# Channel attention over a 384 x 384 x 384 image: 374 rows kept instead of 372, the last folded group in two pieces of three

## The chip, the cores and the metric

The kernel runs on one core of a Trainium2 chip. A core has five engines, each with its own instruction stream: TensorE (PE, matrix products), VectorE (DVE, elementwise work), ScalarE (ACT, functions of one input), GpSimd (POOL) and SyncE (SP), which here does nothing but issue transfers. Transfers between the chip's memory and the on-chip SBUF run on 16 DMA engines. The metric is the device time of one execution in microseconds; the number given is the median of several runs.

## The reference

`x` is `1 x 384 x 384 x 384` in bf16 and `w1d` has one element.

```
g = einsum("bhwc->bc", x) / (H * W)      # mean over all pixels, per channel
s = sigmoid(g * w1d[0])                  # 384 numbers
return x * s[:, None, None, :]
```

All of `x` (113 MB) has to be read before the first output value is known, and 113 MB have to be written. SBUF is far smaller than `x`, so most of `x` has to be read a second time, unless some of it stays in SBUF from the first pass to the second.

## The kernel before

**Layout.** The 147,456 pixels are cut into 1152 *rows* of 128 pixels; a row is 128 partitions x 384 channels, 98,304 bytes (96 KiB). SBUF holds an *arena* of 275 such rows (`ROWS`). In pass one all 1152 rows are loaded and TensorE adds each into one accumulator by a product with a matrix of ones (`sum_rows`, L280). Then ScalarE makes `s` from it (L503). In pass two each row is multiplied by `s` (`scale`, L517) and stored (L531); the rows that no longer lie in SBUF are loaded again (L274).

**Rows kept.** `N_KEPT` rows needn't be loaded again. Some lie in the arena as they are (*raw* rows, `N_RAW`). The others lie *folded*: four blocks of q rows are packed into three, because a part of the bits of each bf16 number is the same throughout. `GROUPS` lists the groups as (first arena row, q). A group of q takes 4q rows when it is loaded and 3q once `fold` is through, and the q rows at its top come free. `fold` handles a *piece* of p rows per block: two tests on ScalarE that the numbers are packable (L352, reading the scratch rows `Y` that VectorE fills), and ten VectorE instructions (L315 on one operand, L321 on two, with the scratch rows `T`). Pass two undoes it with `unfold`: `fields`, `three` and `fourth`, L315 and L321 again, followed by the scaling. One group (`BANKED`, q = 6) spends the time between in TensorE's accumulator memory. The last one, `EXTRA`, lies at A = 220 with q = 4, in one piece. From W = 232 on, up to the end of the arena, come raw rows; `T` and `Y`, the last 16, are raw rows too once all folds are done. U (108 to 115) and V (212 to 219) are the tops of the last groups of the two columns, raw as well.

**Order of pass one.** It is written out by hand, and SyncE, TensorE, ScalarE and VectorE each follow it. `stream_all` loads rows that are only summed; `take` loads a group's rows; `BETWEEN` puts streamed rows between the groups. After the last group, `EXTRA`, come the streamed rows of `LATE`, then the raw rows that stay (`take_raw`). A load waits until the rows that it overwrites are no longer needed: for streamed rows until TensorE has summed them, for the freed top of a group until `fold` has read it, for `T` and `Y` until the last fold is through.

**Padding.** `hold` makes an engine wait several times for a semaphore that has already been reached. `N_DVE = (62, 14)` puts 62 such instructions (two waits each) at the head of VectorE's stream and 14 ahead of the end of pass one; `N_SP = 20` puts 20 into SyncE's stream.

**Order of pass two.** A small planner (the loop from L771) lays out the instructions while the program is built: it steps a clock of 0.05 us with prices for a row's transfer (0.2267 us), for latencies and for VectorE's instructions, and writes down what each engine would do next. `landed` first holds the raw rows for VectorE, `alongside` those that GpSimd scales in the meantime (13 rows: 4, 4 and 5). Rows that have been stored are free (`idle`) and are loaded with streamed rows, the largest free stretch first. `order` is the order in which the groups are unfolded: the last of the first column, then EXTRA, then the one before the last of the first column, and so on. A group can start if its column has no other group in work (`free`) and if the rows at its top (`TOPS`) are free; the tops of the next two groups in line are not loaded (`N_NEAR`). The first two groups are stored in two parts if q is 8 (`apart`). What comes out is a fixed order per engine, with waits on semaphores; on the chip SyncE issues strictly in that order.

Of the kernel before, what the change touches and what calls it, by code (L numbers as in the profile page):

```python
# [145 lines left out]
def kernel(  # L146
# [13 lines left out]
    B, H, W, C = x.shape  # L160
# [11 lines left out]
    PIECE = 4  # L172
    PAIR = 2 * PIECE
    PAIRS = 4
    U = 3 * PIECE + PAIRS * 3 * PAIR
    G0 = U + PAIR
    V = G0 + PAIRS * 3 * PAIR
    A = V + PAIR
    N_A = 39
    T = A + N_A  # L180
    Y = T + 2 * PIECE
# [3 lines left out]
    FIRST = 0  # L185
    GROUPS = [(0, PIECE)]
    COLUMNS = ([FIRST], [])
    for i in range(PAIRS):
        for column, a in zip(COLUMNS, (3 * PIECE, G0)):
            column.append(len(GROUPS))  # L190
            GROUPS.append((a + 3 * PAIR * i, PAIR))
    BANKED = len(GROUPS)
    GROUPS.append((A, 6))
    EXTRA = len(GROUPS)
    GROUPS.append((A, PIECE))
    W = A + 3 * PIECE
    PS = 3 * GROUPS[BANKED][1]
    N_BANKED = 4 * GROUPS[BANKED][1] + 1
    N_RAW = ROWS - W + 2 * PAIR
# [2 lines left out]

    pieces = [
        (g, lo, min(m, q - lo))
        for g, (_, q) in enumerate(GROUPS) for m in [q if g == BANKED else PIECE] for lo in range(0, q, m)
    ]

    ones = pool.tile([P, P], bf16, name="ones")
# [51 lines left out]
    def raw(a):  # L260

        return c_raw + (a - U if a < G0 else PAIR + a - V if a < A else 2 * PAIR + a - W)

# [104 lines left out]
            join(w2, w2, flat(T + i * p, p), XOR, wc[2] + rows(T + i * p, p), wc[2])  # L368


    N_DVE, N_SP = (62, 14), 20

    fl.add("ACT", lambda: nc.scalar.dma_start(out=w_bf[:], in_=w1d.to_broadcast((1, 1))), writes=["w_bf"], dma=True)
    fl.add("DVE", lambda: nc.vector.memset(ones[:], 1.0), writes=["ones"])  # L374
# [35 lines left out]
    def take(g, lo=0, hi=None):  # L410

        a, q = GROUPS[g]
        hi = (N_BANKED if g == BANKED else 4 * q) if hi is None else hi
        load(c_group[g] + lo, a + lo, hi - lo)
        return sum_rows(a + lo, hi - lo)
# [16 lines left out]
    for i, bk in enumerate(banks):  # L432
        lo, hi = i * BANK, min((i + 1) * BANK, PS * C)
# [4 lines left out]
    S1, S2, S3 = ([slot] for slot in SLOTS)  # L438
# [9 lines left out]
    def group(g, where):  # L448

        if isinstance(where, list):  # L450
            take(g)
            for k in of_group(g):
                fold(k)
            stream_all(where)
        else:
            k1, k2 = of_group(g)
            take(g, 0, 12)
            take(g, 24, 32)
            fold(k1)
            stream_all(where[0])  # L460
            take(g, 12, 24)
            fold(k2)
            stream_all(where[1])

    LATE = [(W + 4, 8), (U, 8), (W + 12, 8), (W + 20, 7)]
    BETWEEN = [
        (2, LOW_COLUMN + HIGH), (4, [(A, 38)]),
        (5, [(G0 - 24, 24), (A - 24, 24), *S1]),
        (6, (S2, S3 + S1)), (7, ([(A - 24, 24)] + S2, S3 + S1)),
        (8, (S2 + S1, [(U, 8)] + S3)), (EXTRA, LATE),  # L470
    ]
    between = sum(n for _, b in BETWEEN for w in b for _, n in (w if isinstance(w, list) else [w]))
    first = N_STREAM - between
# [18 lines left out]
        load(raw(a), a, n)  # L492
        return sum_rows(a, n)

    for a, n in [(V, 8), *LATE, (W, 4), (T, 4), (T + 4, 4), (Y, 4), (Y + 4, 2), (Y + 6, 2)]:
        step = take_raw(a, n)
        if a == Y - 4:
            fl.hold("DVE", 2 * N_DVE[1], step)
# [144 lines left out]
    landed = deque()  # L643
# [45 lines left out]
        return f  # L689


    for a, n, end in ((Y, 2, True), (Y + 2, 2, True), (Y + 4, 4, True), (U, 4, True), (U + 4, 4, True), (T, 8, True), (V, 8, True)):
        landed.append((a, raw(a), n, end))
    landed.append((W, raw(W), 8, True))
    landed.append((W + 8, raw(W + 8), 6, True))


    alongside = deque()
    t = 1.0
    for a, n in ((A + 26, 4), (A + 30, 4), (A + 34, 5)):  # L700
        scale(a, n, "POOL", after=[copied])
        t += 0.2 + 0.84 * n
        alongside.append((t, a, raw(a), n))


    (c0, c1), N_NEAR = COLUMNS, 2
    order = [c0[-1], EXTRA, c0[-2], c1[-1], BANKED, c0[-3], c1[-2], c0[-4], c1[-3], FIRST, c1[-4]]
    line = deque(order)
    home = {g: i for i, column in enumerate(COLUMNS) for g in column}
    home[BANKED], home[EXTRA] = 2, 3  # L710
# [60 lines left out]
    while True:  # L771

        if dve_at <= now:
# [4 lines left out]
            if landed and (ahead < PENDING or not can):  # L778
                a, at, n, end = landed.popleft()
# [13 lines left out]
        if alongside and alongside[0][0] <= now:  # L793
            _, a, at, n = alongside.popleft()
# [3 lines left out]
        while waiting and waiting[0][0] <= now:  # L798
            _, n, then, at, a, known = waiting.popleft()
# [10 lines left out]
        if bank_at is None and len(line) <= total - BANKS_AT and got and max(got)[0] >= N_BANKED:  # L810
            a = max(got)[1]
# [11 lines left out]
        if got and todo < N_STREAM:  # L823
            n, a = max(got)
# [60 lines left out]
```

## Time and profile before

| | |
|---|---|
| Median of 3 runs | 719.24 us (718.77 to 719.4) |
| The profiled execution's own time | 718.83 us |
| its span, first to last instruction | 717.1 us |
| moved by the DMA engines | 303.31 MB |
| read, written | 189.92 MB, 113.25 MB |
| VectorE busy | 475.2 us |
| TensorE busy | 213.0 us |
| ScalarE busy | 121.4 us |
| GpSimd busy | 10.2 us |
| s is ready in SBUF | 269.2 us after the start of the span |

The profile's page begins with the busy time of each engine, then cuts the span into 40 equal slices and gives for each the busy share of the engines, of the DMA engines, and the rate that they moved. Other views used below: the busy time of each engine in chosen stretches (windows), the instructions in order of time (timeline), the groups of equal instructions by line and shape with the mean duration of one (nanoseconds), the chain of work that ended last, and the instructions of one source line, for transfers with the time from issue to landing. "128x1536" is four rows wide, since a row has 384 elements per partition; 768 KB in the transfer view are eight rows.

### The profile page before, as it was taken

How to read it: one execution, taken by the hardware profiler on the slowest of the kernel's cores; microseconds unless marked ns; L12 is line 12 of the kernel's file. 1: busy time of each engine (PE TensorE's matmuls, PEld its weight loads, DVE VectorE, ACT ScalarE, POOL GpSimd, SP SyncE). 2: the span in 40 equal slices, each digit the busy share in tenths (PEclk: the TensorE clock that was granted, in tenths of full speed). 3: DMA queues.
4: the chain of work that ended last, by engine and by line, in shares of the span. 5: the costliest groups of instructions: out<-in, count | busy, mean ns of one | idle time of the engine just before them, and what ended most of it. 6: DMA issues, size and time to landing. Idle time of an engine off the chain costs nothing.

```text
span 717.1 us, 2040 instructions
## 1 busy us (share of the span) xinstructions
PE 213.0 (30%) x1186; PEld 0.3 (0%) x3; DVE 475.2 (66%) x355; ACT 121.4 (17%) x97; POOL 10.2 (1%) x7
## 2 busy tenths in 40 slices
PE   4776978998869780000000000000000000000000
PEld 0000000000000000000000000000000000000000
DVE  4606280639896829999999999779966960128900
ACT  3704160426674610000110000000000000000000
POOL 0000000000000005000000000000000000000000
PEclk9998989999999996555555555555555555555555
DMA  9999999999999989999999999999999999999997
GB/s 373 436 426 440 424 442 426 439 429 420 428 430 425 427 358 355 406 424 431 433 428 422 444 424 445 423 439 428 439 420 435 433 433 436 436 432 431 437 421 343
DMA packets 21038, 303.31 MB, mean 423 GB/s; under 512 B 2338, under 2 KB 2850, under 8 KB 9378
## 3 DMA queue, kind: packets, MB, share of 16 engines
q1 hardware_dynamic: 21024, 303.18, 99.1%
q8 instruction: 4, 0.07, 0.0%
q14 instruction: 8, 0.07, 0.0%
q10 hardware_dynamic: 2, 0.00, 0.0%
HBM read 189.92 MB, written 113.25 MB: 423 GB/s over the span
## 4 chain that ended last, share of the span: by engine, by line
DMA 56%; DVE 23%; PE 7%; another core or an unknown queue 3%; ACT 2%; POOL 1%; SPq 1%; issue 0%; DVEq 0%
DMA arena<-in_x_dram 45%; DVE arena L517 17%; DMA out_dram<-arena 11%; PE bank L280 7%; DVE arena L315 4%; ACT arena L352 2%; DVE arena L321 2%; POOL arena L517 1%; SPq L274 1%; SPq L531 0%; ACT s_bf L503 0%; ACT bank L507 0%; ACT bank L429 0%; DVEq L124 0%
## 5 line engine op out<-in xcount | busy, mean ns | idle before, releaser
L517 DVE TENSOR_TENSOR arena<-arena,s_bf 128x6144 bf16<-128x6144 bf16 (+13 forms) x67 | 226.9, 3424 | 86.1 <-DMA arena<-in_x_dram 71.0
L280 PE MATMUL bank<-arena,ones 128*128 128x384 bf16 x1151 | 207.2, 342 | 46.2 <-DMA arena<-in_x_dram 45.6
L315 DVE TENSOR_SCALAR arena<-arena 128x1536 uint16<-128x1536 uint16 (+4 forms) x193 | 136.9, 763 | 107.6 <-DMA arena<-in_x_dram 94.9
L352 ACT ACTIVATE arena<-arena 128x3072 uint16<-128x3072 uint16 (+1 forms) x38 | 107.6, 2831 | 111.6 <-DVE arena L315 111.6
L321 DVE TENSOR_TENSOR arena<-arena 128x1536 uint16<-128x1536 uint16 (+3 forms) x81 | 106.3, 1312 | 8.4 <-PE bank L280 5.2
L597 PE MATMUL bank<-odd,ones 128*128 128x1 bf16 x1 | 0.2, 184 | 262.2 <-DVE odd L592 262.2
L429 ACT COPY arena<-bank 128x512 uint32<-128x512 uint32 (+3 forms) x9 | 4.4, 497 | 86.6 <-DMA out_dram<-arena 86.3
L517 POOL TENSOR_TENSOR arena<-arena,s_bf 128x1536 bf16<-128x1536 bf16 (+1 forms) x3 | 9.9, 3345 | 269.2 <-ACT bank L507 269.2
L517 DVE TENSOR_TENSOR arena<-arena,bank 128x1536 bf16<-128x1536 bf16 (+3 forms) x8 | 9.4, 1248 | 0.0
L429 ACT COPY bank<-arena 128x512 uint32<-128x512 uint32 (+3 forms) x9 | 4.1, 489 | 26.5 <-PE bank L280 26.5
L352 ACT ACTIVATION_READ_ACCUMULATOR arena<-arena 128x1 f32 x38 | 7.1, 186 | 0.0
L280 PE MATMUL bank<-zeros,ones 128*128 128x384 bf16 x32 | 5.5, 326 | 0.0
L503 ACT ACTIVATE s_bf<-bank,w_sc 128x384 bf16<-128x384 f32 x1 | 0.6, 580 | 13.6 <-PE bank L280 13.6
L294 PE MATMUL bank<-arena,ones 128*128 128x384 bf16 x1 | 0.5, 477 | 7.1 <-DMA arena<-in_x_dram 7.1
L853 ACT ACT_TABLE_LOAD x1 | 1.3, 1283 | 0.7 <-PEq L869 0.7
L384 DVE TENSOR_SCALAR w_sc<-bank 128x1 f32<-128x1 f32 x1 | 0.2, 159 | 1.4 <-PE bank L379 1.4
L379 PE MATMUL bank<-w_bf,ones 1*128 1x1 bf16 x1 | 0.2, 183 | 2.4 <-DMA w_bf<-in_w1d_dram 2.4
L374 DVE MEMSET ones<- 128x128 bf16 x1 | 0.2, 165 | 1.0 <-SPq L118 1.0
L601 DVE CAST odd_i<-bank 128x1 int32<-128x1 f32 x1 | 0.2, 159 | 0.3 <-PE bank L597 0.3
L507 ACT COPY bank<-s_bf 128x192 uint32<-128x192 uint32 x1 | 0.3, 323 | 0.0
L597 PEld LDWEIGHTS bank<-odd,ones 128*128 128x128 bf16 x1 | 0.1, 102 | 521.0 <-DVE odd L592 521.0
L587 DVE TENSOR_REDUCE worst<-seen 128x1 f32<-128x38 f32 x1 | 0.2, 184 | 0.0
(8 smaller groups left out, 0.9 us busy)
## 6 DMA issues: line engine op xcount, KB each, us to landing
arena<-in_x_dram SPq DMA_DIRECT2D x18, 4608.0 KB, 31.8
out_dram<-arena SPq DMA_DIRECT2D x9, 4608.0 KB, 34.5
out_dram<-arena SPq DMA_DIRECT2D x7, 3072.0 KB, 23.6
arena<-in_x_dram SPq DMA_DIRECT2D x5, 3072.0 KB, 15.2
arena<-in_x_dram SPq DMA_DIRECT2D x13, 1152.0 KB, 17.1
arena<-in_x_dram SPq DMA_DIRECT2D x6, 2304.0 KB, 20.1
arena<-in_x_dram SPq DMA_DIRECT2D x15, 768.0 KB, 7.7
arena<-in_x_dram SPq DMA_DIRECT2D x2, 4128.0 KB, 38.2
```

The lines of the kernel that those rows point to most:

```text
L274: lambda: nc.sync.dma_start(out=arena[:, a : a + hi - lo, :], in_=view(xf, *run)[:, lo:hi, :]),
L280: return pe.add_instruction(mybir.InstMatmult(name=nc.get_next_instruction_name(), ins=[pe.lower_ap(rhs), pe.lower_ap(ones[:])], outs=[pe. ...
L294: return nc.tensor.matmul(acc, lhsT=ones[:], rhs=arena[:, i, :], start=first, stop=last)
L315: lambda: nc.vector.tensor_scalar(out=dst, in0=src, scalar1=s0, scalar2=s1, op0=op0, op1=op1),
L321: "DVE", lambda: nc.vector.tensor_tensor(out=dst, in0=a, in1=b, op=op), reads=reads, writes=writes
L352: lambda: nc.scalar.activation(out=y, in_=y, func=ACTF.Copy, accum_out=seen[:, 2 * k + i : 2 * k + i + 1]),
L429: "ACT", lambda: nc.scalar.copy(dst.bitcast(u32), src.bitcast(u32)), reads=reads, writes=writes
L503: lambda: nc.scalar.activation(out=s_bf[:], in_=acc, func=ACTF.Sigmoid, scale=w_sc[:, 0:1]),
L507: "ACT", lambda: nc.scalar.copy(s_ps.bitcast(u32), s_bf[:].bitcast(u32)), reads=["s_bf"], writes=["bank0"]
L517: lambda: vec.tensor_tensor(out=v, in0=v, in1=s[:, None, :].to_broadcast([P, n, C]), op=Op.mult),
L597: lambda: nc.tensor.matmul(votes, lhsT=ones[:], rhs=odd[:], start=True, stop=True),
L853: nc.scalar.preload_act_table(ACTF.Sigmoid)
```

## The change

EXTRA gets q = 6: 24 rows are loaded for it, 18 stay. It is folded in two pieces of three rows, and unfolded in two. The rows it frees are W to W + 5, with W = 238. The arena's raw rows become 53 (59 before), folded rows 320 (312), so 374 rows are kept (372) and 778 are loaded twice (780). In pass one EXTRA's rows come in three loads (9, 6 and 9) with eight streamed rows ahead of the last; LATE has 23 streamed rows instead of 31. The raw rows of W are loaded as 4 and 2. In pass two the first raw rows scaled are in another order, W ahead of T, U and V; GpSimd scales 15 rows, in three instructions of five; and EXTRA comes third in line instead of second. VectorE's first hold has 50 instructions instead of 62.

```diff
+    LAST_GROUP = 6
     BANKED = len(GROUPS)
     GROUPS.append((A, 6))
     EXTRA = len(GROUPS)
-    GROUPS.append((A, PIECE))
-    W = A + 3 * PIECE
+    GROUPS.append((A, LAST_GROUP))
+    W = A + 3 * LAST_GROUP
...
-        for g, (_, q) in enumerate(GROUPS) for m in [q if g == BANKED else PIECE] for lo in range(0, q, m)
+        for g, (_, q) in enumerate(GROUPS) for m in [{BANKED: q, EXTRA: q // 2}.get(g, PIECE)] for lo in range(0, q, m)
...
-    N_DVE, N_SP = (62, 14), 20
+    N_DVE, N_SP = (50, 14), 20
...
             k1, k2 = of_group(g)
-            take(g, 0, 12)
-            take(g, 24, 32)
+            q = GROUPS[g][1]
+            take(g, 0, 3 * q // 2)
+            take(g, 3 * q, 4 * q)
             fold(k1)
             stream_all(where[0])
-            take(g, 12, 24)
+            take(g, 3 * q // 2, 3 * q)
             fold(k2)
             stream_all(where[1])
 
-    LATE = [(W + 4, 8), (U, 8), (W + 12, 8), (W + 20, 7)]
+    LATE = [(U, 8), (W + 6, 8), (W + 14, 7)]
...
-        (8, (S2 + S1, [(U, 8)] + S3)), (EXTRA, LATE),
+        (8, (S2 + S1, [(U, 8)] + S3)), (EXTRA, (LATE[:1], LATE[1:])),
...
-    for a, n in [(V, 8), *LATE, (W, 4), (T, 4), (T + 4, 4), (Y, 4), (Y + 4, 2), (Y + 6, 2)]:
+    for a, n in [(V, 8), *LATE, (W, 4), (W + 4, 2), (T, 4), (T + 4, 4), (Y, 4), (Y + 4, 2), (Y + 6, 2)]:
...
-    for a, n, end in ((Y, 2, True), (Y + 2, 2, True), (Y + 4, 4, True), (U, 4, True), (U + 4, 4, True), (T, 8, True), (V, 8, True)):
+    for a, n, end in ((Y, 2, True), (Y + 2, 2, True), (Y + 4, 4, True), (W, 4, True), (W + 4, 2, True), (T, 8, True), (U, 8, True)):
         landed.append((a, raw(a), n, end))
-    landed.append((W, raw(W), 8, True))
-    landed.append((W + 8, raw(W + 8), 6, True))
+    landed.append((V, raw(V), 8, True))
...
-    for a, n in ((A + 26, 4), (A + 30, 4), (A + 34, 5)):
+    for a, n in ((A + 24, 5), (A + 29, 5), (A + 34, 5)):
...
-    order = [c0[-1], EXTRA, c0[-2], c1[-1], BANKED, c0[-3], c1[-2], c0[-4], c1[-3], FIRST, c1[-4]]
+    order = [c0[-1], c0[-2], EXTRA, c1[-1], BANKED, c0[-3], c1[-2], c0[-4], c1[-3], FIRST, c1[-4]]
```

## The prediction

> **What bounds the kernel.** The page comes first: who is busy, and all the time or in stretches?
>
> ```profile
> span 717.1 us, 2040 instructions
> PE 213.0 (30%) x1186; PEld 0.3 (0%) x3; DVE 475.2 (66%) x355; ACT 121.4 (17%) x97; POOL 10.2 (1%) x7
> ...
> DMA  9999999999999989999999999999999999999997
> GB/s 373 436 426 440 424 442 426 439 429 420 428 430 425 427 358 355 406 424 431 433 428 422 444 424 445 423 439 428 439 420 435 433 433 436 436 432 431 437 421 343
> ```
>
> The DMA engines are busy in every slice, VectorE in two thirds of the span: the bound is bytes over the rate of the DMA engines. Only the first slice, slices 15 to 17 and the last fall off. I opened those by windows: per line the stretch, its length, busy time of PE, PEld, DVE, ACT and POOL, then TensorE's clock, the DMA share and the rate.
>
> ```profile
> 250.00:264.00 14.00, 11.77 (x68) 0.00 (x0) 4.72 (x7) 3.87 (x4) 0.00 (x0) 1.00 1.02 420
> 266.00:268.00 2.00, 1.72 (x10) 0.00 (x0) 0.00 (x0) 0.00 (x0) 0.00 (x0) 1.00 0.24 90
> 268.00:270.00 2.00, 0.55 (x4) 0.00 (x0) 0.80 (x2) 0.90 (x2) 0.39 (x1) 1.00 0.01 4
> 284.00:286.00 2.00, 0.00 (x0) 0.00 (x0) 1.97 (x2) 0.00 (x0) 0.00 (x0) 0.50 0.97 265
> 290.00:292.00 2.00, 0.00 (x0) 0.00 (x0) 2.00 (x2) 0.00 (x0) 0.00 (x0) 0.50 0.99 288
> 292.00:340.00 48.00, 0.00 (x0) 0.00 (x0) 46.69 (x36) 0.00 (x0) 0.00 (x0) 0.50 1.02 425
> 340.00:640.00 300.00, 0.18 (x1) 0.10 (x1) 228.85 (x103) 4.37 (x9) 0.00 (x0) 0.50 1.01 432
> ```
>
> From 266 to past 270 next to nothing moves: pass one has ended, s is being made, the first stores begin. At 284 to 286 and 290 to 292 the engines are busy (0.97, 0.99) and move little; their packets are slow, the queue isn't empty. Everywhere else the queue is full at 420 to 432 GB/s. So an edit changes the time in three ways only: bytes, number of transfers, and places where the queue runs dry.
>
> **Bytes.** 780 streamed rows become 778. A row is 98,304 bytes, at 432 GB/s 0.228 us: two rows, **-0.46 us**. Pass one loads 1152 rows before and after.
>
> **Transfers.** One more load in pass one (EXTRA and LATE 6 for 5, the raw rows 11 as before), one store fewer in the raw rows (11 for 12), one more for the group that is now second in line (32 rows, the last but one of the first column), which is stored in two parts. What a transfer costs in a full queue: 14 us at 420 instead of 432 GB/s lose 0.39 us, over some 7.5 transfers of 8 rows, 0.05 us each. **+0.05 us**, 0 to 0.2 with what the planner may cut otherwise.
>
> **The folds at the end of pass one.** Here is the old EXTRA, one piece of four rows, and what SyncE did after it (timeline, chain, two issues).
>
> ```profile
> 247.16 1.90 DVE L315 TENSOR_SCALAR arena<-arena 128x3072 uint16<-128x3072 uint16 x3 [1.00 <-DMA arena<-in_x_dram]
> ...
> 252.93 1.95 DVE L321 TENSOR_TENSOR arena<-arena 128x1536 uint16<-128x1536 uint16 x2
> 255.95 0.40 issue
> L274 SPq DMA_DIRECT2D arena<-in_x_dram x2: 432/432/433, 258.1 to 258.6; - x2
> DMA to landing us min/median/max: 9.4/9.4/9.4
> ```
>
> It ran from 247.16 to 254.88, 7.7 us. SyncE reached the loads that need it at 255.95, after its end, so the fold was hidden; the last load was issued at 258.6 and landed at 268.0, which shows the depth of the queue. The new pieces have these rows:
>
> ```profile
> L315 DVE TENSOR_SCALAR arena<-arena 128x1536 uint16<-128x1536 uint16 x124 | 62.4, 558 | 5.9 <-ACT arena L352 2.8 <-DMA arena<-in_x_dram 1.6
> L321 DVE TENSOR_TENSOR arena<-arena 128x1536 uint16<-128x1536 uint16 x44 | 42.0, 956 | 0.9
> ...
> L315 DVE TENSOR_SCALAR arena<-arena 128x2304 uint16<-128x2304 uint16 x10 | 7.0, 754 | 0.0
> L321 DVE TENSOR_TENSOR arena<-arena 128x2304 uint16<-128x2304 uint16 x4 | 5.4, 1357 | 0.1
> ```
>
> Two rows more are 0.196 us on L315 and 0.40 on L321, so three rows (no row shows that shape) take 0.46 and 0.755. A piece: 0.754 + 6 x 0.46 + 1.357 + 2 x 0.755 = 6.4 us, with gaps 6.6; it is bounded by 7.7, the piece of four. What lies ahead of EXTRA has six rows more (the first stretch of streamed rows grows by six, LATE shrinks by eight, EXTRA grows by eight), so all comes 1.4 us later: the first piece's 15 rows land at 248.3, its fold ends at 254.9, the second (landed by 252.2) runs to 261.5 and has read the freed rows at 260.0, two joins earlier. Waiting for that are the loads of W (4 and 2), and behind them on SyncE's queue those of T and Y. 22 rows come from W on, 5.0 us, so in a full queue their turn is at 263.0; taking off 1.4 us from issue to first byte (below), the deadline is 261.6. Slack 1.6 us. **0**; if each piece takes 7.7 us, u is read at 262.2 and 0.6 us are lost. A gain is excluded, for the queue ahead is full already.
>
> **Padding.** VectorE's holds:
>
> ```profile
> L126 DVEq EVENT_SEMAPHORE  x57: 49/50/50, 2.7 to 8.2; - x57
> L126 DVEq EVENT_SEMAPHORE  x11: 49/50/50, 267.0 to 268.0; - x11
> L126 DVEq EVENT_SEMAPHORE  x3: 50/50/50, 268.4 to 268.6; - x3
> ```
>
> They come 0.098 us apart (57 in 5.5 us), but after the one at 268.0 there is a pause of 0.4. The first hold is at the head, where VectorE waits for the first rows in any case: twelve fewer gain nothing. The extra piece brings ten instructions and two or three waits, so the second hold moves by at most one place and keeps the pause inside (it stood at the 12th of 14). **0**; if the pause slipped behind the hold it would lie on the path from s to the first store, 0.4 us. The Trainium skill's page "Runtime: NRT & Kernel Launch", section "Instruction fetch mechanics", says that instructions are refilled in blocks of 256 and that crossing a block is mostly hidden. Here the pause shows that it isn't hidden among short waits; by the page the term would be 0 in either case.
>
> **The start of pass two.** Rows: VectorE's raw rows (eight from the accumulator memory's copy of s), GpSimd's, the first store and the store of T.
>
> ```profile
> 269.68 9.40 DVE L517 TENSOR_TENSOR arena<-arena,bank 128x768 bf16<-128x768 bf16 x8
> ...
> 278.99 1.93 DVE L315 TENSOR_SCALAR arena<-arena 128x1536 uint16<-128x1536 uint16 x3
> L517 POOL TENSOR_TENSOR arena<-arena,s_bf 128x1920 bf16<-128x1920 bf16 x1 | 3.8, 3825 | 0.0
> L517 DVE TENSOR_TENSOR arena<-arena,bank 128x1536 bf16<-128x1536 bf16 x3 | 2.7, 948 | 0.0
> ...
> L517 DVE TENSOR_TENSOR arena<-arena,bank 128x768 bf16<-128x768 bf16 x1 | 0.5, 546 | 0.0
> L531 SPq DMA_DIRECT2D out_dram<-arena x1: 348/348/348, 269.8 to 269.8; - x1
> DMA to landing us min/median/max: 1.8/1.8/1.8
> L531 SPq DMA_DIRECT2D out_dram<-arena x1: 332/332/332, 274.5 to 274.5; - x1
> DMA to landing us min/median/max: 3.6/3.6/3.6
> ```
>
> The first store, two rows, landed in 1.8 us into an empty queue, 0.46 of it bytes: 1.4 us of latency. T's eight rows, issued at 274.5, had 16 rows of VectorE and 4 of GpSimd ahead of them. In the new order 14 rows of VectorE lie ahead and nothing of GpSimd, whose first piece of five is done at 269.6 + 3.8 = 273.4 and which the planner's clock (piece at 5.4, T at 5.3) puts behind T. T is scaled 0.4 us earlier (546 for 948 ns), issued at 274.1, and can land at 274.1 + 1.4 + 1.85 = 277.35. The 14 rows have landed at 274.9 (271.6 for the first two, 12 more at 0.228 plus 0.05 for each of four transfers and 0.3 of waiting for VectorE), and T behind them in a full queue would land at 276.75. The queue is dry for **+0.6 us**; the bounds are 0 (GpSimd's piece gets ahead after all) and 1.0 (the four rows that lay between). The Trainium skill's page "DMA: Bandwidth & Descriptors", section "Anatomy of one DMA", gives about 2.0 us fixed cost per transfer in place of the 1.4; by it this gap would be 1.2 and the whole 0.6 us worse.
>
> Then VectorE runs out. Its 38 raw rows (46 before) end at 277.4, and the unfolding of the last group writes into U, stored only behind 35 rows: 271.2 + 35 x 0.228 + 0.6 + 0.4 = 280.2. It starts there instead of at 278.99, and its first twelve rows are ready at 288, 1.3 us later than before. What hides this: GpSimd's 15 rows (the last five done at 281.1) and V are still in the queue, and the first loads, 11, 8 and 10 rows into W, V and GpSimd's places, fill it up to about 291. **0**, if those loads go out as they did (first at 280.9).
>
> **The smaller ring.** Until the first group's stores are through, streamed rows circle through the free raw rows. They were V (8), 23 behind EXTRA's top and 4 of the group: 35. Now they are 8, 15 and 4: 27, eight rows or 1.8 us of DMA time fewer. And EXTRA's 16 rows (3.6 us) no longer come between; the second in line shares the first's column, and the planner waits until that has been stored. What the queue had in store:
>
> ```profile
> out_dram<-arena SPq DMA_DIRECT2D x3, 768.0 KB, 8.2
> arena<-in_x_dram SPq DMA_DIRECT2D x2, 768.0 KB, 6.8
> ```
>
> Between 292 and 340 eight rows took 6.8 to 8.2 us to land, 1.4 + 1.85 of it their own: 3.5 to 5 us lay ahead of them. Less 1.8 that leaves 2 to 3 us, and VectorE, with no EXTRA to unfold, answers faster to each landing: on the chip nothing but its place in line holds the second group back, so it can begin while the first is still being stored. Following the instructions by hand I find no store issued later than about 2 us before the queue would need it. **0**, bounds 0 and 2.3 (rival two). VectorE's own extra work, 2 x (3 x 0.46 + 2 x 0.755 + 1.06 + 0.46) = 8.8 us for 5.5 of the one piece of four, lies in a stage where it has 71 us to spare (228.85 of 300).
>
> **Sum**: -0.46 + 0.05 + 0.6 = +0.2 us on the profiled execution's 718.83, that is 719.0. This one lies 0.41 below the median of the runs, 719.24, so the forecast of a median is **719.4**; the likeliest case's own range is 718.6 to 720.2.
>
> **Rivals.** *One: the second piece comes too late and the end of pass one stalls.* For it: three joins in this pass waited for TensorE, 5.2 us in all, the longest 2.2 by the view of waits:
>
> ```profile
> DVE arena L321 <- PE bank L280: 5.2, 3, 2.2
> ```
>
> If both new pieces wait so, 4.4 us against a slack of 1.6 give 2.8: **722.2**. Against it: the old EXTRA's join didn't wait, since its rows had been summed. It decides once the freed rows are read after 261.6. *Two: the ring runs dry.* 4.5 us in store, less 1.8 for the rows, 1.3 for the late first group and 3.6 for EXTRA's absence, is -2.2: **721.6**. Against it: the second group isn't held back on the chip. *Three: the saving alone*, no gap at T: **718.8**. *Four: the two slow stretches vanish with the new sizes.* They lose 2 x (432 - 265)/432 = 0.77 and 0.67 us; without them and without the gap 718.83 + 0.41 - 0.41 - 1.44 = **717.4**. No row shows what made them slow.
>
> **Chances.** Forecast 0.56, rival one 0.11, two 0.16, three 0.11, four 0.06. 0.2% is 1.44 us, about what runs of this kernel can tell from no change. The forecast and three lie within it, and so does a tenth of the others; slower are one and two in most of their sizes; faster is four. That gives 0.06 faster, 0.69 same, 0.25 slower. The range takes in four's better half and two's price: 717.8 to 721.9.
>
> **What would show it.** Right: 778 rows streamed (303.1 MB moved for the 303.3 of before); the loads of W issued at about 260 and the last landing still at 268; a dip of about 0.6 us between 274 and 278; VectorE idle from 277 to 280; a DMA share near 1 from 292 to 340. Wrong: windows between 258 and 266 below 400 GB/s (rival one), or idle DMA engines between 285 and 330 (rival two), or a last store that waits for VectorE at the end, where the sizes of the last streamed loads change as well.

## The result, and the profile after

| | before | after |
|---|---|---|
| Median of 6 runs each, us | 719.29 (718.21 to 719.67) | 722.91 (721.58 to 723.65) |
| The profiled execution, us | 718.83 | 721.58 |
| its span, us | 717.1 | 719.8 |
| SyncE's transfers | 146 | 153 |
| moved, MB | 303.31 | 303.11 |

The ratio is 1.0052, 95% interval 1.0039 to 1.0065: slower. Measured twice more, as u_same and u_again below, the changed kernel gave 1.0027 (1.0018 to 1.0037) and 1.0035 (1.0022 to 1.0049). So the change costs 2 to 3.6 us. The first two of these intervals don't overlap: the cost moves by about a microsecond from one set of runs to another, so below, smaller differences between runs of different sets aren't told apart. The page after begins so (span, busy times, share of the DMA engines and rate per slice):

```profile
span 719.8 us, 2071 instructions
PE 214.9 (30%) x1186; PEld 0.3 (0%) x3; DVE 484.3 (67%) x384; ACT 124.6 (17%) x101; POOL 11.6 (2%) x7
...
DMA  9999999999999988999999999999999999999997
GB/s 375 437 427 435 437 426 429 437 433 423 428 429 427 424 333 341 398 421 422 426 436 424 430 442 427 440 426 439 428 436 423 440 431 438 430 432 427 437 428 321
```

Slices 15 to 17 have 333, 341, 398 for 358, 355, 406, and the last 321 for 343; elsewhere the slices scatter by a few GB/s. VectorE has 9 us more to do, but the DMA engines are the bound as before. The windows tell in which stretch the time went. First the kernel before, then the changed one (columns as in the prediction; the last is the rate, the one ahead of it the DMA share):

```profile
270.00:284.00 14.00, 0.00 (x0) 0.00 (x0) 13.93 (x14) 0.00 (x0) 9.56 (x3) 0.60 0.96 390
284.00:292.00 8.00, 0.00 (x0) 0.00 (x0) 7.88 (x7) 0.00 (x0) 0.00 (x0) 0.50 1.01 354
300.00:320.00 20.00, 0.00 (x0) 0.00 (x0) 18.96 (x18) 0.00 (x0) 0.00 (x0) 0.50 1.02 424
320.00:360.00 40.00, 0.00 (x0) 0.00 (x0) 39.53 (x23) 3.95 (x8) 0.00 (x0) 0.50 1.02 429
```

```profile
270.00:284.00 14.00, 0.00 (x0) 0.00 (x0) 11.58 (x13) 0.00 (x0) 11.31 (x3) 0.55 0.92 372
284.00:292.00 8.00, 0.00 (x0) 0.00 (x0) 6.40 (x4) 0.00 (x0) 0.00 (x0) 0.50 0.90 294
300.00:320.00 20.00, 0.00 (x0) 0.00 (x0) 18.73 (x17) 0.00 (x0) 0.00 (x0) 0.50 1.01 413
320.00:360.00 40.00, 0.00 (x0) 0.00 (x0) 34.33 (x32) 0.00 (x0) 0.00 (x0) 0.50 1.01 425
```

Against 432 GB/s a stretch loses (432 - rate) / 432 of its length: 1.36, 1.44, 0.37, 0.28 us before and 1.94, 2.56, 0.88, 0.65 after. The four rows are 0.58 + 1.12 + 0.51 + 0.37 = 2.6 us worse; 0.3 of the 0.58 is the later end of pass one, for the first store is issued at 270.10 instead of 269.79. The two rows fewer give 0.46 back, and the last slice of this profile takes some 0.9 (22 of 432 GB/s over 18 us), since the 16 DMA engines end further apart (3.6 us for 2.5). That makes 3.0 us, for 2.7 between the spans. From 284 to 292 the engines have idle time, share 0.90; from 300 on they are busy and slow.

The worst stretch, in order of time (timeline of the changed kernel), and what SyncE waited for there, after and before:

```profile
277.75 3.92 SPq L533 DMA_DIRECT2D out_dram<-arena  x3
280.07 2.60 DVE L316 TENSOR_SCALAR arena<-arena 128x1536 uint16<-128x1536 uint16 x3 [2.35 <-DMA out_dram<-arena]
281.79 3.49 SPq L275 DMA_DIRECT2D arena<-in_x_dram  x3
...
290.08 2.36 DVE L519 TENSOR_TENSOR arena<-arena,s_bf 128x4224 bf16<-128x4224 bf16 x1 [1.57 <-DMA arena<-in_x_dram]
```

```profile
SPq L533 <- POOL arena L519: 2.4, 1, 2.4
SPq L533 <- DVE arena L519: 1.3, 1, 1.3
```

```profile
SPq L531 <- DVE arena L517: 1.7, 2, 0.9
```

SyncE stands 2.4 us at the store of GpSimd's third piece; it issues that store at 281.34 and the first load of pass two, of 11 rows, right behind it at 281.79. The store ahead of this pair landed at 283.06, only 1.7 and 1.3 us after the two were issued. The load's bytes take 2.5 us. Counted from the landing of GpSimd's third store, the transfer just ahead (284.11 on the first of the 16 DMA engines, 284.93 on the last), the load landed 0.8 us late on the first engine, at 287.4, and 2.6 us late on the last, at 290.1. VectorE waits 1.57 us for it. Before, GpSimd's third store was issued at 279.58, more than 4 us ahead, and SyncE never waited for GpSimd.

### The profile page after: what moved, and what is told of

Read it like the earlier page. It is cut to its first block, busy times and chain, and to the rows that moved or that the text cites. A ratio compares the mean times of both kernels' runs of the same rounds, so it can differ in the third digit from the quotient of the medians.

```text
span 719.8 us, 2071 instructions
## 1 busy us (share of the span) xinstructions
PE 214.9 (30%) x1186; PEld 0.3 (0%) x3; DVE 484.3 (67%) x384; ACT 124.6 (17%) x101; POOL 11.6 (2%) x7
## 2 busy tenths in 40 slices
DMA packets 22046, 303.11 MB, mean 421 GB/s; under 512 B 2450, under 2 KB 3218, under 8 KB 10130
## 4 chain that ended last, share of the span: by engine, by line
DMA 64%; DVE 19%; PE 6%; ACT 4%; POOL 2%; SPq 1%; issue 0%; DVEq 0%
DMA arena<-in_x_dram 47%; DMA out_dram<-arena 17%; DVE arena L519 13%; PE bank L281 6%; DVE arena L316 5%; ACT arena L353 4%; DVE arena L322 2%; POOL arena L519 2%; SPq L275 1%; SPq L533 0%; ACT s_bf L505 0%; ACT bank L509 0%; ACT bank L430 0%; DVEq L124 0%; SPq L881 0%
## 5 line engine op out<-in xcount | busy, mean ns | idle before, releaser
L519 DVE TENSOR_TENSOR arena<-arena,s_bf 128x6144 bf16<-128x6144 bf16 (+14 forms) x73 | 228.9, 3171 | 87.4 <-DMA arena<-in_x_dram 76.8
L316 DVE TENSOR_SCALAR arena<-arena 128x1536 uint16<-128x1536 uint16 (+6 forms) x210 | 142.4, 731 | 108.1 <-DMA arena<-in_x_dram 95.5
L353 ACT ACTIVATE arena<-arena 128x3072 uint16<-128x3072 uint16 (+2 forms) x40 | 110.5, 2763 | 112.8 <-DVE arena L316 112.8
L322 DVE TENSOR_TENSOR arena<-arena 128x1536 uint16<-128x1536 uint16 (+4 forms) x88 | 109.8, 1247 | 8.8 <-PE bank L281 5.3
L519 POOL TENSOR_TENSOR arena<-arena,s_bf 128x1920 bf16<-128x1920 bf16 x3 | 11.4, 3828 | 269.5 <-ACT bank L509 269.5
L519 DVE TENSOR_TENSOR arena<-arena,bank 128x3072 bf16<-128x3072 bf16 (+2 forms) x7 | 7.7, 1175 | 0.0
```

What stands on the lines that cost most here:

```text
L316: lambda: nc.vector.tensor_scalar(out=dst, in0=src, scalar1=s0, scalar2=s1, op0=op0, op1=op1),
L322: "DVE", lambda: nc.vector.tensor_tensor(out=dst, in0=a, in1=b, op=op), reads=reads, writes=writes
L353: lambda: nc.scalar.activation(out=y, in_=y, func=ACTF.Copy, accum_out=seen[:, 2 * k + i : 2 * k + i + 1]),
L519: lambda: vec.tensor_tensor(out=v, in0=v, in1=s[:, None, :].to_broadcast([P, n, C]), op=Op.mult),
```

## The experiments

The letters in the expectations are theories. A: the loss comes from the first loads of pass two (their place or size). B: from the new order and the smaller ring of free rows. C: from the folds in two pieces, or from the address distance between partitions, 735 rows for 737 in the second run of streamed rows. D: from the padding. F: a *short lead*, a load that is issued too shortly before the engines have nothing left. G: the kept rows or folds as such. R: the reload of a slot in the ring is issued too late. Every ratio is to runs of the kernel before on the same chip; its median was 719.1 to 719.5 us in each set of runs. The sets are, in the order of the table, the first four runs, the next four, the next four, three, and two.

| run | median us (range, runs) | ratio, 95% interval |
|---|---|---|
| b_order | 720.04 (719.25 to 720.24, 10) | 1.0005 (0.9995 to 1.0014) |
| rows_only | 720.9 (719.18 to 722.21, 8) | 1.0021 (1.0009 to 1.0033) |
| u_pool | 721.86 (721.06 to 723.66, 6) | 1.0039 (1.0026 to 1.0051) |
| u_pad | 721.67 (721.07 to 722.42, 7) | 1.0029 (1.0017 to 1.0040) |
| u_same | 721.51 (720.37 to 722.4, 10) | 1.0027 (1.0018 to 1.0037) |
| u_stride | 721.93 (720.57 to 722.33, 9) | 1.0029 (1.0019 to 1.0039) |
| b_stride | 720.01 (719.24 to 720.87, 11) | 1.0006 (0.9997 to 1.0015) |
| u_six_five | 721.96 (721.61 to 722.23, 6) | 1.0032 (1.0020 to 1.0044) |
| b_pool15 | 719.82 (719.14 to 720.46, 11) | 1.0006 (0.9996 to 1.0015) |
| b_ring | 721.67 (721.34 to 722.26, 7) | 1.0030 (1.0019 to 1.0042) |
| u_ahead | 726.3 (725.78 to 726.88, 5) | 1.0097 (1.0082 to 1.0111) |
| b_split | 719.89 (719.2 to 720.71, 11) | 1.0005 (0.9996 to 1.0014) |
| b_ring4 | 719.86 (718.82 to 720.57, 11) | 1.0008 (0.9999 to 1.0017) |
| u_late4 | 721.48 (720.21 to 722.27, 7) | 1.0029 (1.0018 to 1.0041) |
| b_small | 720.16 (719.34 to 721.54, 11) | 1.0016 (1.0007 to 1.0025) |
| u_again | 721.71 (721.12 to 722.68, 5) | 1.0035 (1.0022 to 1.0049) |
| rows_late4 | 720.77 (719.95 to 722.99, 11) | 1.0026 (1.0016 to 1.0036) |

**One part alone: order, rows, GpSimd, padding.** b_order is the kernel before with EXTRA third in line; the other three are the changed kernel with parts undone.

```diff
# b_order (from before)
-    order = [c0[-1], EXTRA, c0[-2], c1[-1],
+    order = [c0[-1], c0[-2], EXTRA, c1[-1],
# u_pad (from after)
-    N_DVE, N_SP = (50, 14), 20
+    N_DVE, N_SP = (62, 14), 20
# u_pool (from after)
-    for a, n in ((A + 24, 5), (A + 29, 5), (A + 34, 5)):
+    for a, n in ((A + 26, 4), (A + 30, 4), (A + 34, 5)):
# rows_only (from after): order, GpSimd's 13 rows and the list of raw rows as before
```

> The kernel before with one edit: EXTRA (still q = 4) third in line instead of second. Theory A (the loss lies at the first loads of pass two, 283 to 293 us, where single DMA engines stand on packets four times as long as usual; it depends on how the first loads are lined up): those are the same as before here, so 719.3, within 0.2% of before. Rival B (the new order: more and smaller transfers and a ring of fewer rows, a loss spread over 295 to 355 us): slower, 721 to 723.

> The changed kernel with the order of the groups, the order of VectorE's raw rows and GpSimd's 13 rows as before; 374 rows, q = 6 in two pieces and the padding stay. Theory A: the first loads of pass two are 8, 8 and 8 to 10 rows as before, so 719 to 719.8. Rival C (the folding in two pieces, or the other strides of the rows in memory, 349 and 735 instead of 347 and 737, slow the transfers): 722 to 723.5, as the changed kernel.

> The changed kernel with GpSimd's pieces as before (4, 4, 5) and the two rows scaled by VectorE as a last raw piece. The first loads become other ones (W with fewer rows of GpSimd's). Theory A: somewhere between, 719.5 to 722.9, and the loss that is left shows in the landings of the first loads. Rival B: no change to 722.9.

> The changed kernel with 62 waits again at the head of VectorE's stream. Theory A and rivals B and C: no change to the changed kernel, 722.5 to 723.3. Rival D (the place of the instruction fetches, which share the DMA engines, costs the time): back to 719.5 or so.

The order alone costs nothing that can be told (its interval ends at 1.0 us), and so does the padding (u_pad against u_same). rows_only, without the edits at the start of pass two, keeps about 1.4 us of the loss, which is in neither theory's range, and has it in another place:

```profile
284.00:292.00 8.00, 0.00 (x0) 0.00 (x0) 7.38 (x6) 0.00 (x0) 0.00 (x0) 0.50 1.02 389
300.00:320.00 20.00, 0.00 (x0) 0.00 (x0) 19.72 (x26) 0.00 (x0) 0.00 (x0) 0.50 1.01 392
```

From 284 to 292 it moves more than the kernel before (354), from 300 to 320 less (424), and less than the changed kernel (413). There VectorE is busy for 19.72 of 20 us; EXTRA, second in line again and unfolded in two pieces, begins at 308.6. Whether the smaller ring or the busier VectorE slows that stretch, no run separates. In u_pool the stretch 284 to 292 has 336 GB/s for 294, but it has 8 transfers more than the changed kernel, and its median is no better.

**Distance and size of the first loads.** u_same is the changed kernel again; u_stride and b_stride move the border between the two runs of streamed rows (43 rows) to 41 and 45; u_six_five cuts the first load in two.

```diff
# u_stride (from after); b_stride has 45 (from before)
-    N_FIRST = 43
+    N_FIRST = 41
# u_six_five (from after)
-            n = min(n, CAP, left)
+            n = min(n, CAP if todo >= 1 else 6, left)
```

> The changed kernel again, beside which the next three are read. Its profile showed 2.6 us lost on the first load of pass two (11 rows, 8448 bytes per packet: the first DMA engine had it at 287.4 us, the last at 290.1). If that belongs to the program, the load is late by 2 to 3 us again and the time is 721.5 to 723.5 us, 1.003 to 1.005 of before; if it was the chance of one execution, the load is late by under 1 us in this profile and the time still 2 to 3 us above before.

> The changed kernel with the first run of streamed rows 41 long, so that the second run has 737 rows per partition as before and not 735. Theory C (the address distance between partitions makes the reads slow): 719.2 to 720.5 us, the first loads lose 1.5 us as before. Theory A (the size of the first load after the stores decides): no change, 721.5 to 723.5 us with 3 us or more lost on the first loads.

> The kernel before with the first run 45 rows long, so that the second has 735 rows per partition as in the changed kernel; everything else is as before. Theory C: 1 to 2.5 us slower than before, 720.5 to 722 us. Theory A: within 0.5 us of before.

> The changed kernel with its first load of pass two, 11 rows, cut into one of 6 and one of 5 rows (155 transfers for 153; the planner's own stall stays 5.95). Theory A (a large first read after a long row of writes is what is slow): the first loads lose 1.5 us as before and not 3.5, so 720 to 721 us, 1.5 to 2 us under the changed kernel of this call. Theory C or chance: no better than the changed kernel, 722 to 723 us.

The worst stretch in the windows of u_stride, u_six_five and b_stride:

```profile
284.00:292.00 8.00, 0.00 (x0) 0.00 (x0) 6.72 (x4) 0.00 (x0) 0.00 (x0) 0.50 0.89 318
```

```profile
284.00:292.00 8.00, 0.00 (x0) 0.00 (x0) 7.36 (x6) 0.00 (x0) 0.00 (x0) 0.50 0.96 320
```

```profile
284.00:292.00 8.00, 0.00 (x0) 0.00 (x0) 7.93 (x7) 0.00 (x0) 0.00 (x0) 0.50 1.01 348
```

The loss of the first load is neither chance nor distance nor size: it is there in u_same, u_stride and u_six_five, with a first load that reaches the last engine 2.3 to 2.6 us late in each (counted as above), and isn't there in b_stride, whose time, 0.7 us above before, lies between its two ranges. Theory C's distance and A's size fall. What these three have in common, beside the rest of the change, is the late issue.

**Is it the lead?** b_pool15 gives the kernel before GpSimd's 15 rows; b_ring takes one slot of 8 rows out of its ring in pass one, so that the ring has 23 rows, as in the changed kernel, and not 31; u_ahead lets the first load go ahead of GpSimd's third store; b_split adds nine transfers.

```diff
# b_pool15 (from before; the last raw rows of VectorE are 4 for 6)
-    for a, n in ((A + 26, 4), (A + 30, 4), (A + 34, 5)):
+    for a, n in ((A + 24, 5), (A + 29, 5), (A + 34, 5)):
# b_ring (from before)
-    LATE = [(W + 4, 8), (U, 8), (W + 12, 8), (W + 20, 7)]
+    LATE = [(U, 8), (W + 12, 8), (W + 20, 7)]
-    for a, n in [(V, 8), *LATE, (W, 4),
+    for a, n in [(V, 8), *LATE, (W + 4, 8), (W, 4),
# u_ahead (from after)
-(todo or not (landed or alongside or waiting))
+(todo or not (landed or len(alongside) > 1 or waiting))
# b_split (from before)
-        load(streamed[0], a, n)
+        for lo in (0, 24) if n == 48 else (0,):
+            load(streamed[0] + lo, a + lo, 24 if n == 48 else n)
```

> The kernel before with 15 rows on GpSimd in 5, 5, 5 (VectorE scales two rows fewer there); nothing of the folding or of pass one is changed. Theory F (short lead: GpSimd's third store comes 1.7 us later, the first loads stand behind it in SP's queue, and are then issued under 2.5 us before the DMA engines have nothing left, so that their packets are slow): the third store and the first load together lose 2.5 to 3.3 us where before they lost 0.7 (the first three loads together 1.5), and the time is 1 to 2.3 us above before. Theory G (the loss comes from the 374 kept rows or from the folds): within 0.5 us of before, the first loads lose 1.5 us as before. The planner's own stall is 4.9 for 4.55 and there are 3 more transfers, 0.2 us in both cases.

> The kernel before with 23 rows in the ring of the last loads of pass one and not 31: the slot of 8 rows at W + 4 is left out of it and loaded once. Pass two is as before. Theory F: the load of 8 rows at row 244 is issued 1.3 to 1.9 us and not 3 us before the first DMA engine runs out, and it and the next one lose 0.2 to 1 us, as in the profiles of the changed kernel; the time is 0 to 1 us above before. Theory G: no loss there, the time within 0.3 us of before.

> The changed kernel with the first load of pass two (11 rows) allowed ahead of GpSimd's third store: it is planned at 10.55 and not 14.2. The planner cuts the next loads otherwise and puts its own stall at 8.4 for 5.95. Theory F: the first load is issued 4 us or more before the engines run out and with the third store loses under 1 us where the changed kernel lost 3.2; the time falls by 1 to 2 us, to 719.5 to 721 us, unless what is now third in line runs short in turn (then 721 to 723 us, with the loss at 288 to 295 us). Theory G: the loss stays where it was, 721.5 to 723 us.

> The kernel before with each load of 48 rows in pass one made as two of 24, nine transfers more with the same bytes; pass two is as before. If a transfer in a full queue costs 0.06 us, as fitted on the landings of both kernels, the last load of pass one lands 0.5 to 0.6 us later and the time is 0.3 to 0.8 us above before; if transfers cost nothing beside their bytes, within 0.2 us.

b_pool15's windows:

```profile
284.00:292.00 8.00, 0.00 (x0) 0.00 (x0) 6.34 (x5) 0.00 (x0) 0.00 (x0) 0.50 0.95 319
300.00:320.00 20.00, 0.00 (x0) 0.00 (x0) 19.23 (x18) 0.00 (x0) 0.00 (x0) 0.50 1.02 422
320.00:360.00 40.00, 0.00 (x0) 0.00 (x0) 39.52 (x24) 0.00 (x0) 0.00 (x0) 0.50 1.02 433
```

The slow first load appears as foreseen (the store and the load lose 2.6 us on the last engine), and the stretch loses 0.65 us by the rate. But the time rises by 0.5 only, which is theory G's mark (within 0.5) and not theory F's (1 to 2.3), and the interval takes in no change at all. From 300 to 360 the rates are those of before within a few GB/s. So the loss on the last engine overstates what such a load costs the kernel before; the stretch's 0.65 us is within the interval. The last engine falls behind early instead of later: in the kernel before the first and last engine land 0.4 us apart at 290 and 2.5 at the end; in b_pool15 2.1 and 3.1.

b_ring is the find. Only pass one was changed, by one slot, and it loses 2.3 us, more than either theory allowed (0 to 1 us). SyncE's waits from 246 to 258, before, in b_ring and in b_ring4 (below), and the last load of pass one in b_ring (issued at 260.7, landed at 270.2; before 258.6 and 268.0):

```profile
SPq L274 <- PE bank L280: 7.4, 5, 3.4
```

```profile
SPq L274 <- PE bank L280: 8.9, 5, 3.4
```

```profile
SPq L274 <- PE bank L280: 6.4, 7, 2.5
SPq L274 <- DVE arena L321: 0.2, 1, 0.2
```

```profile
L274 SPq DMA_DIRECT2D arena<-in_x_dram x1: 450/450/450, 260.7 to 260.7; - x1
...
DMA to landing us min/median/max: 9.4/9.4/9.4
```

u_ahead is the slowest run, where theory F had it gain 1 to 2 us. Its first load went out early (279.5), and landed late:

```profile
L275 SPq DMA_DIRECT2D arena<-in_x_dram x1: 1115/1115/1115, 279.5 to 279.5; - x1
...
DMA to landing us min/median/max: 10.9/10.9/10.9
```

The loads behind it came too late (the fourth was issued at 291.5, when the third had landed on the first engine at 291.4), and the DMA engines had idle time:

```profile
284.00:288.00 4.00, 0.00 (x0) 0.00 (x0) 3.93 (x4) 0.00 (x0) 0.00 (x0) 0.50 0.92 300
288.00:292.00 4.00, 0.00 (x0) 0.00 (x0) 2.58 (x2) 0.00 (x0) 0.00 (x0) 0.50 0.87 361
292.00:296.00 4.00, 0.00 (x0) 0.00 (x0) 3.34 (x3) 0.00 (x0) 0.00 (x0) 0.50 0.88 266
...
330.00:340.00 10.00, 0.00 (x0) 0.00 (x0) 8.24 (x5) 0.00 (x0) 0.00 (x0) 0.50 0.86 323
```

The first load itself speaks against theory F. It was issued 4.3 us before the store ahead of it had landed on the first engine (283.8; in the changed kernel 2.3 us, in the kernel before 4.9). Still it landed on the first engine at 287.2 and on the last at 290.4, 3.5 us late there, and some of its packets took up to 1.7 us, where 0.32 is usual for their size. In rows_only, issued 4.0 us ahead, the first load lost nothing on the last engine; in b_pool15, 3.7 us ahead, it lost about 2 us. In the changed kernel the late issue goes with idle engines (a share of 0.57 from 284 to 285), but that it makes the packets of the first load slow isn't shown, and what does stays open.

b_split's last load of pass one landed at 268.4, 0.4 us later for nine transfers; the median rises by 0.55, with an interval that takes in no change. That would be 0.05 to 0.06 us for each, the price that the prediction took, but it isn't clear of the scatter: landings of one and the same pass one differ by 0.7 us between profiles (below).

**What the ring costs, and where.** b_ring4 and u_late4 load the ring of pass one in pieces of four rows, so that a reload waits for half as many sums; b_small keeps 8 rows out of the ring of pass two in the kernel before.

```diff
# b_ring4 (from b_ring); u_late4 the same with its own LATE (from after)
-    LATE = [(U, 8), (W + 12, 8), (W + 20, 7)]
+    LATE = [(U, 4), (U + 4, 4), (W + 12, 4), (W + 16, 4), (W + 20, 4), (W + 24, 3)]
# b_small (from before)
-                    idle[i] = True
+                    idle[i] = not 236 <= i < 244
...
+        if 40 <= todo < 40 + 48 and not late:
+            late.append(1)
+            release(236, 8)
         got = runs()
```

> As b_ring (the kernel before with a ring of 23 rows at the end of pass one, 721.67 us), but the ring's loads are of four rows and not eight: a slot's reload waits for the sums of four rows, 0.75 us less, and there are 6 transfers more than in b_ring, 0.4 us. Theory R (the reload of a slot is issued too late, because landing, sums and issue take as long as 23 rows take to stream): the reloads are issued 2 us or more and not 1.4 us before the first DMA engine runs out, the last load of pass one lands 1 us or more earlier than b_ring's 270.2 us, and the time is 719.5 to 721 us. If something else of b_ring costs the 2.3 us (the order of the last loads), 721.5 to 722.5 us.

> The changed kernel with the loads of its ring at the end of pass one in pieces of four rows: 6 transfers more, 0.4 us; pass two is planned as in the changed kernel. Theory R: the loss at 255 to 264 us (0.1 to 1.0 us in the profiles so far, 0.5 on the mean) goes, the last load of pass one lands at 268.0 to 268.4 us, and the time is 721.5 to 722.5 us, since transfers take back what the reloads gain and the loss at the start of pass two stays. If the ring of pass one were the whole of the change's loss, it would be 720 to 721 us.

> The kernel before with 8 rows (236 to 243) kept out of the ring of pass two until 41 rows have been loaded: 27 rows go round as in the changed kernel. There are 9 more transfers (0.5 us), and the planner's own stall is 5.2 for 4.55. Theory R: loads at 290 to 310 us are issued under 2.5 us before the engines run out, packets are slow there, and the time is 720.5 to 723 us, 0.5 to 3 us more than its transfers explain. If the ring of pass two costs nothing, as the prediction had it: 719.7 to 720.2 us, the transfers alone.

With the same 23 rows in smaller pieces 1.6 to 1.8 of b_ring's 2.3 us are gone, though it has 6 transfers more: theory R holds for b_ring. The loop of a slot is landing, sums of the whole piece, issue, first byte. Between a slot's load and its reload come the rest of the ring and V's eight rows: in b_ring 31 rows, 31 x 0.228 = 7.1 us of streaming, but U's load and its reload land on the first engine 8.4 us apart (248.49 and 256.87). In the kernel before it is 39 rows, 8.9 us, and W + 4's are 9.1 apart (246.58 and 255.64). In the changed kernel EXTRA's last nine rows lie between U and its reload, so that only two of the three slots come round after 31 rows; W + 6's land 7.9 us apart (251.66 and 259.55). Here is the last load of pass one in the changed kernel, then in u_late4:

```profile
L275 SPq DMA_DIRECT2D arena<-in_x_dram x2: 442/483/524, 261.4 to 261.9; - x2
...
DMA to landing us min/median/max: 6.4/6.4/6.4
```

```profile
L275 SPq DMA_DIRECT2D arena<-in_x_dram x2: 431/432/433, 261.1 to 261.6; - x2
...
DMA to landing us min/median/max: 6.6/6.6/6.7
```

They land at 268.3 and 268.2. In the nine profiles with the changed pass one (the changed kernel three times, u_pad, u_stride, u_six_five, u_pool, u_ahead, rows_only) it was 268.3 to 269.1, 268.7 on the mean; in the five with the old one (before, b_order, b_stride, b_pool15, b_small) 268.0 to 268.7, 268.2 on the mean: 0.5 us. That pieces of four rows take it away here isn't shown: u_late4 lands at 268.2, but rows_late4 (below), with the same pass one, at 268.5, and u_late4's time stays at 721.5. By the landings the ring of pass one isn't the main part.

b_small's 720.16 lies inside the range that was named for a ring of pass two that costs nothing (719.7 to 720.2). It is 1.0 us slower than before, 0.5 of it the price of 9 transfers; the other half isn't told apart from 0 (the interval is 0.5 to 1.8 us in all). What points to this ring is how far ahead SyncE issues. For transfers issued between 292 and 312, the time from the issue to the landing, on the first engine, of the transfer ahead was 3.3 to 7.3 us in the kernel before, 3.5 to 8.4 in b_order, 2.7 to 8.6 in b_small, 2.2 to 5.2 in the changed kernel and 1.4 to 6.7 in rows_only; the rates from 300 to 320 were 424, 425, 416, 413 and 392 GB/s. Less time ahead goes with a lower rate, and the new order with the old ring (b_order) has neither. That is an argument from five profiles, not an experiment that changes this alone.

**Do the parts add up?** rows_late4 is rows_only with the ring of pass one in pieces of four; u_again is the changed kernel once more, measured beside it.

> The changed kernel once more, as the anchor for the next run: by its two measurements 721.5 to 722.9 us, 1.0027 to 1.0052 of before. Loss of its first loads of pass two 2.3 to 2.6 us on the slowest DMA engine, as in all profiles of it.

> The changed kernel with three of its parts undone or mended: order, raw rows and GpSimd's 13 rows at the start of pass two as before, and the ring of pass one reloaded in pieces of four rows. What stays are 374 rows, the last group of six in two pieces, the smaller ring of pass two and 16 transfers more than before. From the single parts (rows_only 1.5 us above before, of which 0.5 were the ring of pass one, and 6 transfers more at 0.06): 720.3 to 721 us. If the time is 721.5 us or more, the single parts don't add up and the account by places is wrong.

rows_late4 came out where the sum of its parts puts it, 1.5 us above before by the medians. That is a weak test: in the sum the ring's 0.5 us and the six transfers' 0.4 nearly cancel, and rows_only stood at 1.4. It is 0.9 us below u_again; u_late4, which differs from it in the edits at the start of pass two alone, stands 2.3 us above before by the medians, 0.8 more, but its ratio is 1.0029 for 1.0026. The intervals overlap in both comparisons, so these edits cost somewhere between 0 and 1 us on top. Two windows of u_again show the losses where the first profile had them:

```profile
284.00:292.00 8.00, 0.00 (x0) 0.00 (x0) 6.91 (x5) 0.00 (x0) 0.00 (x0) 0.50 0.91 311
300.00:320.00 20.00, 0.00 (x0) 0.00 (x0) 18.64 (x16) 0.00 (x0) 0.00 (x0) 0.50 1.01 403
```

## Why the prediction was wrong

It said 719.4 us, no change to be told, and 717.8 to 721.9; the median was 722.91. The two later medians, 721.51 and 721.71, lie within the upper end of that range, but all three are slower than before by more than their intervals. What failed are two terms that were put at 0, the first loads of pass two (284 to 292 lost 1.1 us more than before) and the smaller ring (300 to 360 lost 0.9 us more), and a term that is missing, the ring of `LATE` (about 0.5 us). By its own steps, for two of which these windows of the changed kernel are needed:

```profile
250.00:264.00 14.00, 11.00 (x61) 0.00 (x0) 9.52 (x17) 7.39 (x8) 0.00 (x0) 1.00 1.00 389
...
274.00:278.00 4.00, 0.00 (x0) 0.00 (x0) 3.72 (x3) 0.00 (x0) 4.00 (x2) 0.50 1.05 429
```

- **Bytes**, -0.46: right, 303.11 MB.
- **Transfers**, +0.05: b_split doesn't speak against the price; the count was wrong. The planner cut pass two otherwise than the hand count had it, 153 transfers for 146: by that price 0.4 us, so the saving was spent here already.
- **Folds at the end of pass one**, 0: right for the folds. A piece took 6.1 us (6.6 foreseen), the freed rows' loads went out at 258.5 and 258.9 (260 foreseen), and the last load landed at 268.3. But its sign of rival one appeared, 389 GB/s in 250 to 264 for 420, from another cause: this step looked at what EXTRA's folds hold up and not at what the same edit does to `LATE`, whose ring falls from 31 rows to 23. That cost has no term in the sum. By the landings it is about 0.5 us here; in b_ring, where all three slots come round too soon, 2.2.
- **Padding**, 0: right; VectorE's pause of 0.45 us again fell inside the second hold (268.2 to 268.7). It stands ahead of the same instruction in both traces, the 320th that is recorded of VectorE; before, the first hold had one too (0.5 us), ahead of the 64th, 256 earlier.
- **The gap at T**, +0.6: it didn't come. In SyncE's order GpSimd's first store stands ahead of T (273.79 and 274.42), as the lower bound had it; 274 to 278 ran at 429 GB/s. The first store, two rows into an empty queue, landed 1.9 us after its issue, 1.4 beyond its bytes, as before.
- **VectorE runs out at 277.4 and starts again at 280.2**: it was 277.7 and 280.07. **0, if those loads go out as they did (first at 280.9)**: this step failed, by its own condition. The cover named was GpSimd's 15 rows; but with 38 raw rows in place of 46, SyncE had nothing else to issue and stood 2.4 us at the third of them, with all first loads behind it in its queue. The first went out at 281.8, the engines had idle time (a share of 0.57 from 284 to 285), and 284 to 292 lost 1.1 us more than before. Part of that are slow packets, and u_ahead, where the load goes out at 279.5 and its packets are slow all the same, leaves their cause open. In b_pool15, where VectorE still has 44 raw rows, SyncE waited 0.8 us for the same piece:

```profile
SPq L531 <- POOL arena L517: 0.8, 1, 0.8
```

- **The smaller ring**, 0 with bounds to 2.3: the value taken was too low, as far as the places tell. That 2 to 3 us would still lie ahead of a transfer came true (2.2 us at the least); that this costs nothing didn't: the stretches from 300 to 360 are 0.9 us worse in the changed kernel. b_small leaves about 0.5 us beyond its transfers, not told apart from 0, so the cause is argued and not shown.
- **Rivals.** Two (the ring runs dry, 721.6) was nearest in place and price. Its sign, idle engines, showed only at 284 to 287; from 300 to 320 the engines are busy and slow. One, three and four fell. That the two slow stretches of before might vanish (four) was the wrong way round: the first of them became worse.

The sum with what the runs showed: -0.46 for bytes, 0.4 for transfers, 0.5 for the ring of pass one, 0.5 for that of pass two, 0.5 for GpSimd's rows (b_pool15) make 1.4 us of the 2 to 3.6 measured. The last two terms aren't told apart from 0. The rest is open; whether a slow first load costs more in a ring that is already small, no run separates.

## What to carry to other kernels

Where a queue is kept full by slots that go round, compare the slot's loop (landing, use of the whole piece, issue, first byte) with the time that the ring takes to stream, for every phase that the edit touches, not only for the one it is about; where they are nearly equal, smaller pieces can do in place of more slots, as in b_ring4. A queue that issues strictly in order needs work ahead of any wait on a slow helper: ask what is behind that wait when the other work gets less. And before slow transfers are laid to a late issue, issue them early: in u_ahead they stayed slow.

## What the runs showed of the hardware

A busy DMA engine isn't a fast one. In the changed kernel 256 to 264 has a DMA share of 0.99 and 363 GB/s, in u_late4, with reloads issued earlier, 1.03 and 412. The first load of pass two had packets of up to 1.4 us in the changed kernel, for 8448 bytes that take 0.32 on the median, and of up to 1.7 us in u_ahead, though it was issued 2.3 us ahead in the one and 4.3 us in the other; in the kernel before, 4.9 us ahead, its packets of 6144 bytes took at most 0.34 (median 0.23). So the lead alone doesn't tell slow packets from fast ones. The Trainium skill's page "DMA: Bandwidth & Descriptors", section "Latency and other measured facts", gives the memory's access latency as 0.2 us on average and 2 us at high load; that would fit such packets, but no run here measures the latency by itself.

The 16 engines don't keep step: they land the same transfer 0.2 us apart in the stores after s, mostly 2 to 2.5 us in pass one, and 2.5 to 4.4 us at the end of these kernels. Each transfer is done when the last engine is, so this spread is paid at the end; in b_pool15 2.1 us of it was there at 290, in the kernel before it grew between 300 and 640, and both ended within 0.5 us.
